# Strassen jobs in another product order over six PSUM banks, two gate/up tiles ahead instead of four, and a new table of kept-back halves

## The chip, the cores and the metric

One Trainium2 chip, one core of it. The metric is device time in microseconds (us) of one execution of the kernel; a median of several runs is compared. TensorE multiplies, VectorE (DVE in the profile) and GpSimd (POOL) work element by element, ScalarE (ACT) evaluates functions and copies, SyncE (SP) issues most of the transfers. "us" is microseconds throughout.

## The reference, cut to what matters

```python
x = A_x                                   # (1, 2048, 512)
xn = layernorm(x)
# A: attention, 32 heads of 16
qkv = xn @ wqkv                           # 512 x 1536
p = softmax(q @ k.T * 16 ** -0.5)         # per head, 2048 x 2048
s = (p @ v).reshape(1, 2048, 512) @ wo
# B: SwiGLU
h = silu(xn @ w_gate) * (xn @ w_up)       # 512 x 1792
g = silu(h @ w_down)                      # 1792 x 512
return x + s * g
```

## The kernel before, in words

The 2048 tokens are four blocks `b` of 512 columns; the 1792 hidden features of B are 14 tiles `f` of 128 (`GROUPS`: tiles 0 to 6 and 7 to 13). A product in near-float32 precision is three matmuls in the type fp32r: high part by high part, low by high, high by low. So every operand is split: ScalarE casts the high part, VectorE subtracts it to get the low part (`whole_of`, `summed_of`, `split_turn`, `split_gu`).

The program has two halves.

**Prologue.** Tokens are normalised and turned, and the values of all blocks and the queries and keys of blocks 0 and 1 are made in plain products (`value_tile`, `feature_tile`). In `value_tile` the twelve matmuls of a tile run chunk by chunk `c`: high·high, low·high, high·low. The queries and keys of blocks 2 and 3, and the gate and up products of the tiles in `AHEAD` for blocks 2 and 3, come from `strassen(i)`, one call per job of the list `jobs`. A job is a 2 x 2 block product in seven products of six matmuls instead of eight products: a pair of query or key tiles (`("qk", pair)`) or one gate/up tile (`("f", f)`), for the two token blocks at once. `product(bank, left, right, start, stop)` issues six matmuls into a PSUM bank; four of the products open a bank, three are added to a bank that is already open. In between, ScalarE copies two of the partial sums to SBUF (`m1`, `m5`), VectorE and GpSimd make the sums `w`, `u3`, `c12`, `c21`, `c22`, and the operands of the next job are split (`sums`, `whole_of`, `summed_of`). In each job the four banks are four tiles of the pool `pps`, and the products run in the order bank 0, bank 1, bank 0 again, bank 2, bank 3, bank 2 again, bank 3 again. The second product into bank 0 has to follow ScalarE's copy `m1` of it, and so on.

A "qk" job ends in four calls of `feature_out`: ScalarE squares (L972) and casts (L973) a 128x512 result, VectorE or GpSimd subtracts (L974) into a tile `parts` (pool `p3`, four buffers), SP stores it (L976), and VectorE keeps a running maximum `top` (L977). Two of the four calls are put off into the next job (`behind`). An "f" job ends in ScalarE's Tanh and VectorE's products into `g1` and `g2` and two stores to `h_d` (L1039, L1044). `bound` multiplies the eight maxima `top` by a small matrix (L820, the "squares") and reduces the two banks; `spread_shift` turns the sum, makes a flag and a shift from it; `first_loads` issues twenty loads of the first keys, values and queries on SP's queue (L186, L203). They are hung into the middle of jobs through the argument `between`. `fill(n)` issues `n` steps of the feed-forward part: a step is a pair of 64-row matmuls side by side (L291). After the last job stands `fill(3 * DC)`, 24 steps, which is the whole first gate unit. Then every engine reads the flag and branches around a general path (`tc.If`, L1132).

**Attention.** `plan()` cuts the 32 units (a group of four heads and a token block, 16 key tiles each) into blocks of `k` key tiles (2 to 6), and gives each block a number `n` of feed-forward steps; it is a cheapest path over a cost per block, whose ends are the ends of the feed-forward units of `SEQUENCE`. In a block, TensorE makes the scores (L1224), ScalarE the exponentials (L1227 for both halves at once, L1234 for one half), the feed-forward steps lie in between, and `values` (L526) multiplies the block before by the values. `SHARED[(k, n)]` lists, for one kind of block, the pairs of which one half is kept back: VectorE copies that half out of PSUM (L1231), and ScalarE exponentiates it from SBUF at the block's end (L1244). The second entry of `SHARED` says after which pair how many steps are issued.

Feed-forward units are gates (24 steps, one tile `f` for one block) and downs (21 steps). For blocks 2 and 3 the tiles in `AHEAD` are left out of `SEQUENCE` and loaded from `h_d` by `load_hidden`. `split_gu` makes the operands of the next gate, `load_gu` loads the one after.

SP issues its transfers in the order of the program; each engine works through its own instructions in order too.

Of the kernel before, what the change touches and what calls it, by code (L numbers as in the profile page):

```python
# [19 lines left out]
P = 128  # L20
# [21 lines left out]
AHEAD = (0, 1, 7, 8)  # L42


def sequence():
# [87 lines left out]
def tile_block(ctx: ExitStack, tc: tile.TileContext, x, xcols, wqkv, wo, w_gate, w_up, w_down, out):  # L133
# [166 lines left out]
    def gate_unit(i, b, f, then):  # L300
        if i + 1 < len(gates):
            split_gu(i + 1)
        if i + 2 < len(gates):
            load_gu(i + 2)
        hi, lo = gu.pop(i)
        n = 0
        for c in range(DC):
            for wt, j in ((hi, 0), (hi, 1), (lo, 0)):
                both(wt[:, c], fx[:, j, c], n == 0, n == 3 * DC - 1)
                n += 1  # L310
                if n == 3 * DC:
                    th = one.tile([P, TB], F32, tag="th", name="th")
                    ga = two.tile([P, TB], F32, tag="ga", name="ga")
                    act(th, bankx, AF.Tanh, scale=0.5)
                    dve.scalar_tensor_tensor(ga, th, 1.0, bankx, op0=ALU.add, op1=ALU.mult)
                    dve.scalar_tensor_tensor(ga, ga, 0.5, banky, op0=ALU.mult, op1=ALU.mult)
                    kept.append((f, ga))
                    if now >= 0:
                        split_kept()
                    then()  # L320
                if n == DC:
                    split_wd()
                if n in (12, 20):
                    split_hidden()
                yield
# [273 lines left out]
    with ExitStack() as pro:  # L599
# [281 lines left out]
        def value_tile(b, t):  # L881
            xh, xl = xt[b % 2]
            order = None
            if b == 0:
                parts = [slice(i, i + 1) for i in range(3)] if t == 1 else [slice(0, 3, 2), slice(1, 2)]
                order = [(i, part) for part in parts for i in range(DT)]
                if t == 1:
                    order.insert(11, (partial(turn_x, 0, 2), None))
# [30 lines left out]
        for at, pair in zip((0, 1, 3, 5), (0, 2, 1, 3)):  # L919
            jobs.insert(at, ("qk", pair))  # L920
# [58 lines left out]
        behind = []  # L979

        def strassen(i, between=None):
# [4 lines left out]
            m1, w, m5, u3, c12, c21, c22, g1, g2 = spots  # L986
# [10 lines left out]
            bank = [pps.tile([P, 512], F32, tag="ps", name="ps") for _ in range(4)]  # L997
            more = i + 1 < len(jobs)
# [3 lines left out]
            nc.scalar.copy(m1, bank[0])  # L1002
            while behind:
                behind.pop(0)()
            product(bank[1], summed[1], t2, True, True)
# [3 lines left out]
            product(bank[0], whole[2], b21, False, True)  # L1009
            if kind == "f":  # L1010
                act(g1, bank[0], AF.Tanh, scale=0.5)
                dve.scalar_tensor_tensor(g1, g1, 1.0, bank[0], op0=ALU.add, op1=ALU.mult)
            else:
                feature_out(2 * f, 2, bank[0], False)
# [9 lines left out]
            else:  # L1024
                split_gu(0)
# [4 lines left out]
            product(bank[2], summed[3], b22, False, True)  # L1030
            dve.tensor_add(c12, bank[2], w)
            if kind == "f":
                act(g2, c12, AF.Tanh, scale=0.5)
            else:
                feature_out(2 * f, 3, c12, False)
            if kind == "f":
                dve.scalar_tensor_tensor(g2, g2, 1.0, c12, op0=ALU.add, op1=ALU.mult)
                dve.scalar_tensor_tensor(g2, g2, 0.5, c22, op0=ALU.mult, op1=ALU.mult)
                sp.dma_start(h_d[1, f], g2)  # L1039
            product(bank[3], whole[0], t4, False, True)  # L1040
            dve.tensor_add(c21, bank[3], w)
            if kind == "f":
                dve.scalar_tensor_tensor(g1, g1, 0.5, c21, op0=ALU.mult, op1=ALU.mult)
                sp.dma_start(h_d[0, f], g1)  # L1044
            else:
                behind.append(partial(feature_out, 2 * f + 1, 3, c22, True))
                behind.append(partial(feature_out, 2 * f + 1, 2, c21, False))
# [6 lines left out]
        step(28, 0, dve.tensor_sub, upper_x, upper_x, lower_x)  # L1054
        step(28, 1, split_turn, 0, upper_x)
        step(29, 0, split_turn, 1, lower_x)
        step(29, 0, whole_of, 0)
# [8 lines left out]
        for b in range(NB):  # L1066
# [4 lines left out]
            for n, (make, i) in enumerate(slots):  # L1071
# [10 lines left out]
                if at == 26:  # L1082
                    dve.memset(acc, 0.0)
# [18 lines left out]
        spots = [spots[:, i] for i in range(4)] + [xin[:, i] for i in range(4)] + [wide_mr[:, 0]]  # L1102
        def spread_shift():
            nc.tensor.transpose(extra[0:1, :P], sm, ident)
            dve.reduce_max(s4, extra[0:1, :P], axis=AX.X)
# [59 lines left out]


# [176 lines left out]
```

## Time and profile before

| | |
|---|---|
| median of 3 runs | 1408.86 us (1408.38 to 1410.98) |
| the profiled execution | 1408.27 us, of it 1406.5 us span |
| TensorE | busy 98% of the span, mean granted clock 0.992 |
| ScalarE, VectorE, GpSimd | busy 84%, 58%, 11% |
| first Strassen product | at 102.86 us |
| first score | at 209.08 us |

Two times lie around a span: the span counts from the first to the last instruction of the program, the run's time some 1.8 us more. In the views a row reads: start, duration, engine, line, operation, out<-in, count, and in brackets how long the engine had stood idle and what ended that. "PEclk" is the granted share of TensorE's clock. A busy TensorE in the table of engines is not one at its peak, since the matmuls overlap; distances between starts say more.

### The profile page before, as it was taken

How to read it: one execution, taken by the hardware profiler on the slowest of the kernel's cores; microseconds unless marked ns; L12 is line 12 of the kernel's file. 1: busy time of each engine (PE TensorE's matmuls, PEld its weight loads, DVE VectorE, ACT ScalarE, POOL GpSimd, SP SyncE). 2: the span in 40 equal slices, each digit the busy share in tenths (PEclk: the TensorE clock that was granted, in tenths of full speed). 3: DMA queues.
4: the chain of work that ended last, by engine and by line, in shares of the span. 5: the costliest groups of instructions: out<-in, count | busy, mean ns of one | idle time of the engine just before them, and what ended most of it. 6: DMA issues, size and time to landing. Idle time of an engine off the chain costs nothing.

```text
span 1406.5 us, 27374 instructions
## 1 busy us (share of the span) xinstructions
PE 1383.1 (98%) x10912; PEld 845.4 (60%) x10912; DVE 820.4 (58%) x1296; ACT 1181.3 (84%) x1971; POOL 157.4 (11%) x192
## 2 busy tenths in 40 slices
PE   9998979999999999999999999999999999999998
PEld 7876756565655556555656565555555565565655
DVE  7697855653644655455646554555556445556656
ACT  6746618889988998999899999999998989989885
POOL 4235620000000000000010100000100000000142
PEclk9999989999999999999999999999999999999999
DMA  9888657254324443434543446246433113225652
GB/s 305 271 273 247 179 146 176 66 110 104 88 64 111 117 103 78 105 83 106 114 109 97 99 104 140 57 90 144 93 67 87 35 38 77 58 74 148 212 179 86
DMA packets 141908, 170.18 MB, mean 121 GB/s; under 512 B 13913, under 2 KB 85617, under 8 KB 141006
## 3 DMA queue, kind: packets, MB, share of 16 engines
q1 hardware_dynamic: 134238, 143.04, 40.6%
q0 software_dynamic: 7056, 24.78, 5.4%
q8 instruction: 88, 1.44, 0.4%
q10 hardware_dynamic: 480, 0.54, 0.1%
q14 instruction: 46, 0.38, 0.1%
HBM read 119.78 MB, written 46.41 MB: 118 GB/s over the span
## 4 chain that ended last, share of the span: by engine, by line
PE 81%; ACT 3%; DVE 1%; issue 0%; DVEq 0%
PE acc L526 30%; PE bankx L291 24%; PE score L1224 9%; PE single L1224 8%; PE banky L291 7%; ACT pr L1234 1%; ACT pr L1244 1%; PE spare L1224 1%; ACT pr L1227 1%; DVE pr L1231 0%; DVE y L296 0%; PE spare L1279 0%; ACT th L295 0%; PE banky L1279 0%; DVE gul L221 0%
## 5 line engine op out<-in xcount | busy, mean ns | idle before, releaser
L526 PE MATMUL acc<-pr,vst 128*17 128x512 f32 x4096 | 460.2, 593 | 0.0
L1234 ACT ACTIVATE pr<-single 128x512 f32<-128x512 f32 x675 | 388.2, 607 | 17.2 <-PE single L1224 10.5
L1227 ACT ACTIVATE pr<-score 128x1024 f32<-128x1024 f32 x335 | 345.9, 1033 | 31.6 <-PE score L1224 19.9
L526 PEld LDWEIGHTS acc<-pr,vst 128*17 128x17 f32 x4096 | 109.7, 97 | 282.5 <-issue 280.1
L291 PE MATMUL bankx<-fx,guh 64*128 64x512 f32 x768 | 254.9, 394 | 3.7 <-PEq L1132 3.7
L291 PE MATMUL banky<-fx,guh 64*128 64x512 f32 x768 | 254.6, 393 | 0.0
L1231 DVE COPY pr<-spare 128x512 f32<-128x512 f32 x177 | 122.3, 691 | 221.4 <-PE spare L1224 203.2
L1244 ACT ACTIVATE pr<-pr 128x512 f32<-128x512 f32 x419 | 230.2, 641 | 0.0
L1224 PE MATMUL score<-qst,kst 50*128 50x512 f32 x847 | 228.8, 418 | 1.4 <-SPq L1132 1.4
L1231 DVE COPY pr<-single 128x512 f32<-128x512 f32 x242 | 166.5, 688 | 97.6 <-PE single L1224 96.4
L1224 PE MATMUL single<-qst,kst 50*128 50x512 f32 x917 | 218.9, 398 | 0.7 <-DVE pr L1231 0.6
L291 PE MATMUL bankx<-wd,hh 64*128 64x512 f32 x672 | 200.1, 392 | 0.0
L291 PE MATMUL banky<-wd,hh 64*128 64x512 f32 x672 | 199.7, 392 | 0.0
L1224 PEld LDWEIGHTS score<-qst,kst 50*128 50x128 f32 x847 | 103.0, 184 | 130.2 <-ACT pr L1234 94.6
L1234 ACT ACTIVATE pr<-score 128x512 f32<-128x512 f32 x177 | 106.1, 599 | 71.9 <-PE spare L1224 58.2
L291 PEld LDWEIGHTS bankx<-fx,guh 64*128 64x128 f32 x768 | 143.7, 187 | 21.8 <-issue 4.7
L291 PE MATMUL bankx<-fx,gul 64*128 64x512 f32 x384 | 151.3, 394 | 0.0
L291 PE MATMUL banky<-fx,gul 64*128 64x512 f32 x384 | 151.3, 394 | 0.0
L291 PEld LDWEIGHTS banky<-fx,guh 64*128 64x128 f32 x768 | 143.8, 187 | 2.8
L1224 PEld LDWEIGHTS single<-qst,kst 50*128 50x128 f32 x917 | 115.6, 185 | 29.1 <-ACT pr L1234 12.3
L291 PEld LDWEIGHTS bankx<-wd,hh 64*128 64x128 f32 x672 | 124.4, 186 | 13.0
L291 PEld LDWEIGHTS banky<-wd,hh 64*128 64x128 f32 x672 | 125.2, 186 | 3.4
(262 smaller groups left out, 1838.8 us busy)
## 6 DMA issues: line engine op xcount, KB each, us to landing
fx<-xt_d SPq DMA_DIRECT2D x48, 512.0 KB
kst<-k_d SPq DMA_DIRECT2D x192, 64.0 KB
qst<-q_d SPq DMA_DIRECT2D x192, 64.0 KB
gur<-in_B_w_gate_dram SPq DMA_DIRECT2D x48, 256.0 KB
gur<-in_B_w_up_dram SPq DMA_DIRECT2D x48, 256.0 KB
q_d<-parts SPq DMA_DIRECT2D x16, 512.0 KB
k_d<-parts SPq DMA_DIRECT2D x16, 512.0 KB
xt_d<-xt POOLq DMA_DIRECT2D x6, 1024.0 KB, 6.5
```

The lines of the kernel that those rows point to most:

```text
L291: mm(bank, lhs[h], rhs[h], start=start, stop=stop)
L526: mm(acc[h * 32:h * 32 + DH + 1], v[:, kt % CT, h * (DH + 1):(h + 1) * (DH + 1)], probs[2 * i + h // 2][:, h % 2], start=tiles[0] == at == ...
L1224: mm(banked[h], k[r, j, kc * P:(kc + 1) * P], q[r, j], start=True, stop=True)
L1227: exps.append(act(pr, both_banks, AF.Exp, scale=0.25))
L1231: dve.tensor_copy(pr[:, h], banked[h])
L1234: exps.append(act(pr[:, h], banked[h], AF.Exp, scale=0.25))
L1244: exps.append(act(part, part, AF.Exp, scale=0.25))
```

## The change

Two tiles, 0 and 7, are computed ahead instead of four, so the job list shrinks from eight jobs (qk, qk, f, qk, f, qk, f, f) to six (qk, qk, f, qk, qk, f), and `SEQUENCE` gains a gate unit each for tiles 1 and 8 of blocks 2 and 3. The seven products run as bank 0, 1, 2, 3, then 0, 2, 3 again, over a ring of six banks: four of `pps`, `extra` and `acc`. Three of the four `feature_out` calls of a "qk" job are put off. In the last job the gate unit 0 is issued in two halves of 12 steps between its fifth product and its last two, `bound` and `spread_shift` lie in this job, and what is left of its results (`first_half`, `second_half`) follows after the branch. `first_loads` moves from job 5, the last "qk" job, to job 3, the last but one, and in the new order it stands ahead of that job's own four results. `acc` is zeroed after the branch. `value_tile` takes high·high and high·low of all chunks first in the first tile of blocks 2 and 3. The table `SHARED` is new.

```diff
-AHEAD = (0, 1, 7, 8)
+AHEAD = (0, 7)
 SHARED = {
-    (2, 6): ((), (0, 0, 1, 5)),
     (3, 9): ((2, 3), (0, 0, 0, 3, 2, 4)),
-    (4, 15): ((2, 5), (0, 0, 1, 3, 3, 2, 2, 4)),
-    (5, 18): ((2, 3, 5, 6, 7), (0, 0, 1, 2, 3, 2, 2, 2, 2, 4)),
-    (5, 21): ((3, 4, 5, 6, 7), (0, 0, 2, 3, 1, 3, 4, 0, 4, 4)),
-    (5, 24): ((2, 3, 7), (0, 0, 0, 4, 1, 5, 5, 2, 3, 4)),
-    (6, 21): ((2, 3, 4, 5, 7, 8, 9), (0, 0, 1, 2, 2, 1, 3, 2, 2, 1, 3, 4)),
+    (4, 15): ((2, 4, 5), (0, 0, 1, 3, 3, 1, 3, 4)),
+    (5, 18): ((2, 3, 5, 6, 7), (0, 0, 3, 1, 3, 2, 2, 1, 2, 4)),
+    (5, 21): ((2, 3, 7), (0, 0, 1, 2, 2, 5, 2, 3, 2, 4)),
+    (5, 24): ((2,), (0, 0, 1, 2, 4, 2, 5, 3, 2, 5)),
+    (6, 21): ((2, 4, 5, 7, 8, 9), (0, 0, 0, 3, 3, 1, 3, 2, 2, 1, 3, 3)),
     (6, 24): ((2, 5, 7, 8, 9), (0, 0, 0, 3, 3, 3, 2, 3, 2, 2, 2, 4)),
 }
 ...
     def gate_unit(i, b, f, then):
-        if i + 1 < len(gates):
+        if 0 < i < len(gates) - 1:
             split_gu(i + 1)
 ...
         def value_tile(b, t):
-            if b == 0:
-                parts = [slice(i, i + 1) for i in range(3)] if t == 1 else [slice(0, 3, 2), slice(1, 2)]
+            if b == 0 or b > 1 and t == 0:
+                parts = [slice(i, i + 1) for i in range(3)] if b == 0 and t == 1 else [slice(0, 3, 2), slice(1, 2)]
 ...
-        for at, pair in zip((0, 1, 3, 5), (0, 2, 1, 3)):
+        for at, pair in zip((0, 1, 3, 4), (0, 2, 1, 3)):
             jobs.insert(at, ("qk", pair))
 ...
         def strassen(i, between=None):
-            bank = [pps.tile([P, 512], F32, tag="ps", name="ps") for _ in range(4)]
+            if not ring_of:
+                free = [pps.tile([P, 512], F32, tag="ps", name="ps") for _ in range(4)]
+                homes_of = {(4 * len(jobs) - 4) % 6: extra, (4 * len(jobs) - 1) % 6: acc}
+                ring_of.extend(homes_of[n] if n in homes_of else free.pop(0) for n in range(6))
+            bank = [ring_of[(4 * i + n) % 6] for n in range(4)]
 ...
             if more:
                 sums(i + 1)
             product(bank[0], whole[1], b11, True, False)
-            nc.scalar.copy(m1, bank[0])
+            product(bank[1], summed[1], t2, True, True)
             while behind:
                 behind.pop(0)()
-            product(bank[1], summed[1], t2, True, True)
+            nc.scalar.copy(m1, bank[0])
             dve.tensor_add(w, bank[1], m1)
             if more:
                 whole_of(i + 1)
-            product(bank[0], whole[2], b21, False, True)
-            ... (the results of bank 0)
+            else:
+                split_gu(0)
             product(bank[2], summed[0], t1, True, False)
             nc.scalar.copy(m5, bank[2])
             if between:
                 between()
             product(bank[3], summed[2], t3, True, False)
             ... (u3, c22, summed_of(i + 1), load_raw or load_gu)
+            if more:
+                product(bank[0], whole[2], b21, False, True)
+                if kind == "f":
+                    first_half()
+                else:
+                    feature_out(2 * f, 2, bank[0], False)
+                product(bank[2], summed[3], b22, False, True)
+                other_half()
+                product(bank[3], whole[0], t4, False, True)
+                second_half()
+                if kind != "f":
+                    behind.append(partial(feature_out, 2 * f + 1, 3, c22, True))
+                    behind.append(partial(feature_out, 2 * f, 3, c12, False))
+                    behind.append(partial(feature_out, 2 * f + 1, 2, c21, False))
+            else:
+                product(bank[2], summed[3], b22, False, True)
+                other_half()
+                fill(3 * DC // 2)
+                spread_shift(ring_of[(4 * i + 4) % 6])
+                split_gu(1)
+                fill(3 * DC // 2)
+                product(bank[0], whole[2], b21, False, True)
+                product(bank[3], whole[0], t4, False, True)
+                behind.append(first_half)
+                behind.append(second_half)
 ...
-                if at == 26:
-                    dve.memset(acc, 0.0)
 ...
-            strassen(i, {0: partial(store_x, 2), 1: partial(store_x, 3), 5: first_loads, 6: bound, 7: spread_shift}.get(i))
-        fill(3 * DC)
+            strassen(i, {0: partial(store_x, 2), 1: partial(store_x, 3), 3: first_loads, len(jobs) - 1: bound}.get(i))
         fast = nc.values_load(flag, min_val=0, max_val=1)
 ...
+        while behind:
+            behind.pop(0)()
+        dve.memset(acc, 0.0)
```

`first_half` is Tanh and one VectorE operation on bank 0 into `g1`, `second_half` is the sum `c21` and for an "f" job one more product and the store of `g1`; `other_half` is the sum `c12`, and for an "f" job Tanh, two products and the store of `g2`.

More of the change, by code (lines that the diff above doesn't have):

```diff
@@ L995, in product, with first_half, second_half, other_half @@
                         n += 1
[L997 to L998 removed]
+            def first_half():
+                act(g1, bank[0], AF.Tanh, scale=0.5)
+                dve.scalar_tensor_tensor(g1, g1, 1.0, bank[0], op0=ALU.add, op1=ALU.mult)
+            def second_half():
+                dve.tensor_add(c21, bank[3], w)
+                if kind == "f":
+                    dve.scalar_tensor_tensor(g1, g1, 0.5, c21, op0=ALU.mult, op1=ALU.mult)
+                    sp.dma_start(h_d[0, f], g1)
+            def other_half():
+                dve.tensor_add(c12, bank[2], w)
+                if kind == "f":
+                    act(g2, c12, AF.Tanh, scale=0.5)
+                    dve.scalar_tensor_tensor(g2, g2, 1.0, c12, op0=ALU.add, op1=ALU.mult)
+                    dve.scalar_tensor_tensor(g2, g2, 0.5, c22, op0=ALU.mult, op1=ALU.mult)
+                    sp.dma_start(h_d[1, f], g2)
             if more:
@@ L1029, in strassen @@
                 load_gu(i + 3 - len(jobs))
[L1030 to L1033, printed above, removed]
-            else:
[L1035 to L1047, printed above, removed]
+            if more:
+                product(bank[0], whole[2], b21, False, True)
+                if kind == "f":
+                    first_half()
[9 more added lines that the diff above has]
+                    behind.append(partial(feature_out, 2 * f + 1, 2, c21, False))
+            else:
+                product(bank[2], summed[3], b22, False, True)
[8 more added lines that the diff above has]
+                behind.append(second_half)
         lower_x, upper_x = xin[:, :2], xin[:, 2:]
@@ L1101, in tile_block, with spread_shift @@
         spots = pc.tile([P, 4, TB], F32, tag="vl", name="spots")
[L1102 to L1105, printed above, removed]
+        spots = [spots[:, i] for i in range(4)] + [xin[:, i] for i in range(4)]
+        def spread_shift(to):
+            nc.tensor.transpose(to[0:1, :P], sm, ident)
+            dve.reduce_max(s4, to[0:1, :P], axis=AX.X)
             dve.tensor_scalar(s4, s4, 0.51, None, op0=ALU.mult)
```

17 lines of the change are left out of this document (8 added, 9 removed).

## The prediction

> **What bounds the kernel now.** I read the page first, then busy time by stretch, then TensorE's waits in the prologue, last the timeline around them. Attention, by stretch (columns: length; busy time of TensorE, its weight loads, VectorE, ScalarE, GpSimd; granted clock, DMA share, GB/s):
>
> ```profile
> 300.00:500.00 200.00, 200.00 (x1708) 116.00 (x1705) 102.43 (x157) 181.75 (x304) 7.20 (x12) 1.00 0.43 99
> ```
>
> TensorE has no hole there, at full clock; ScalarE stands at 91%. Two pieces of the chain that ended last:
>
> ```profile
> 341.55 5.28 PE acc L526 x48
> 355.54 5.28 PE acc L526 x48
> ```
>
> Blocks of six key tiles with 24 steps (the planner's kind (6, 24)) repeat every 13.99 us, 5.28 of it `values`. The prologue is different; a row is one job, the last one is gate unit 0 and the branch:
>
> ```profile
> 102.86:116.64 13.78, 11.54 (x44) 8.96 (x43) 9.13 (x11) 5.49 (x9) 1.75 (x1) 0.88 0.73 200
> ...
> 138.54:148.28 9.74, 9.74 (x44) 7.87 (x42) 8.90 (x14) 4.75 (x9) 5.83 (x6) 1.00 0.69 217
> 148.28:159.06 10.78, 9.94 (x43) 7.81 (x42) 8.64 (x13) 6.56 (x11) 6.98 (x7) 1.00 0.78 204
> ...
> 180.99:197.40 16.41, 12.63 (x46) 9.26 (x44) 8.53 (x16) 2.92 (x5) 2.61 (x3) 0.79 0.60 172
> 197.40:209.08 11.68, 6.60 (x54) 4.89 (x53) 6.03 (x9) 0.60 (x1) 3.78 (x4) 0.93 0.38 105
> ```
>
> ```profile
> PE ps L993 <- ACT spots L1016: 4.8, 2, 3.8
> PE bankx L291 <- PEq L1132: 3.7, 1, 3.7
> PE ps L993 <- DVE spots L1020: 2.5, 3, 0.9
> PE ps L993 <- ACT spots L1002: 2.2, 1, 2.2
> ```
>
> The undisturbed fourth job takes 9.74 us for 42 matmuls, 0.232 each. The eight take 94.5 us (102.86 to 197.40) where 77.9 would do. The waits (total, times, longest) say why: a second product into a bank waits for the copy or sum of the first (L1002, L1016, L1020), and after a long wait the clock is down (0.88, 0.79). So a matmul or step costs 0.232 us everywhere, and the prologue's waits are the stock from which something can be gained.
>
> **The change part by part.** *Two jobs out, four gate units in.* Out: 2 x 9.74 = 19.5 us. In: 4 x 24 = 96 steps. In the block above 13.99 - 5.28 - 12 score slots x 0.232 leaves 5.93 for 24 steps; 5.57 are the steps, 0.36 the block's own overhead. So +22.3 us, and nothing covers it, since TensorE is the engine without holes.
>
> *The planner.* Worked through with the new list, `plan()` gives 103 blocks instead of 107, and 357 kept-back halves instead of 419. Four overheads less: -1.4. Kind (6, 21) falls from 15 blocks to 5, (5, 21) rises from 14 to 27, (5, 24) from 3 to 9. In a (6, 21) block the chain runs from ScalarE's and VectorE's work into a score:
>
> ```profile
> 702.48 0.92 ACT pr L1227
> ...
> 710.09 0.61 DVE pr L1231
> 710.74 0.50 PE spare L1224
> ```
>
> The score at 710.74 waits for the copy; I put such a wait at 0.3 us (half the copy), an estimate, and ten blocks fewer at -3. Bounds: -6 (the whole copy each) and +22 (the second rival). The new gates' splits and Tanh lie under TensorE (VectorE is busy 102 of 200 us). Attention: +22.3 - 1.4 - 3 = +17.9.
>
> *First tile of block 2.* Its low parts are now needed after eight matmuls.
>
> ```profile
> 80.00 0.50 PE L815 MATMUL ps<-vh,xt 128*128 128x512 f32 x1 [1.61 <-DVE xt L743]
> ...
> 81.14 0.73 PE L815 MATMUL ps<-vh,xt 128*128 128x512 f32 x1 [0.17 <-DVE xt L743]
> 81.66 0.63 PE L815 MATMUL ps<-vl,xt 128*128 128x512 f32 x1
> ```
>
> The last low part still comes at 81.1, so the last matmul starts there and not at 81.7: the first job starts 0.6 us earlier, at 102.3. Bounds: 0 and 1.8, the two waits together.
>
> *Six banks, new order.* A second product into a bank now comes four products (5.6 us) after the first. The waits on `spots` were for one copy or sum; the longest that no late transfer made was 2.2, so 5.6 covers them. What is late next: VectorE, filled to 8.6 to 8.9 of 9.74 us a job, which makes the next operands. I leave 0.3 for it (bounds 0 and 1.1 a job, the excess of the fifth job, as the third rival).
>
> *`first_loads` in job 3.* This step speaks against the change. In program order SP now has job 2's stores, the twenty loads, the load of gate 0, and only then the four stores of job 3's `parts`. Before:
>
> ```profile
> 164.07 0.34 SPq L1044 DMA_DIRECT2D h_d<-facc x1
> 166.27 0.37 SPq L976 DMA_DIRECT2D k_d<-parts x1
> 166.69 3.20 SPq L186 DMA_DIRECT2D kst<-k_d x6
> ...
> 177.00 0.73 SPq L213 DMA_DIRECT2D gur<-in_B_w_gate_dram x1
> 177.78 0.62 SPq L213 DMA_DIRECT2D gur<-in_B_w_up_dram x1
> ```
>
> An "f" job's last store is issued 5.0 us into the next job (164.07 against 159.06); 0.4 later the loads start and take 10.3 (166.69 to 177.00), the gate's 1.4. So the first `parts` store goes out 17.1 us into job 3, 7.4 into job 4. How long a store holds its buffer in so full a queue:
>
> ```profile
> 184.71 0.34 SPq L1044 DMA_DIRECT2D h_d<-facc x1
> ...
> 190.89 0.60 ACT L1011 ACTIVATE facc<-ps 128x512 f32<-128x512 f32 x1 [7.66 <-DMA h_d<-facc]
> ```
>
> 6.2 us. `parts` has four buffers; the fifth cast, job 4's first result, is wanted at about 7.7 (six products after five are 7.0, then a square) and waits until 13.6, which is 3.9 into the last job. Behind it on ScalarE stand that job's three put-off results, and after their last maximum come the squares of `bound`:
>
> ```profile
> 172.39 0.63 ACT L972 ACTIVATE sq<-facc 128x512 bf16<-128x512 f32 x1 [0.39 <-DVE facc L1041]
> 172.93 0.60 ACT L973 CAST parts<-facc 128x512 fp32r<-128x512 f32 x1
> ...
> 175.41 0.38 PE L820 MATMUL banky<-top,ind 128*32 128x512 bf16 x1 [0.45 <-DVE top L977]
> ```
>
> A square and a cast take 1.15 (172.39 to 173.53), so ScalarE's last cast starts 3.9 + 0.6 + 3 x 1.15 - 0.6 = 7.4 into the last job, and 2.5 later (172.93 to 175.41) the last square can go: 9.9. TensorE is there after three products, at 4.2. I take 5.6 us of waiting; bounds 0.4 (this wait before) and 7.7 (ScalarE's longest wait for a store).
>
> *The clock.* Before, the last long wait left the clock at 0.79 over 16.41 us, which is 3.4 lost. I take 2.5 for the new one, since part of it falls into idle time; bounds 0 and 3.4. The Trainium skill, "TensorE: Matmul & The Clock Gate", Part 1, says that the clock falls to half after an idle window of some 3.4 us, free-running. By that rule a wait broken into pieces under 3.4 us would cost nothing, and the sum would be 2.5 lower. The trace differs: the 2.2 us wait on L1002 was followed by a job at 0.88, and I go by the trace.
>
> *Gate 0 and the branch.*
>
> ```profile
> 202.85 0.39 PE L291 MATMUL bankx<-fx,gul 64*128 64x512 f32 x1
> ...
> 206.96 0.46 PE L291 MATMUL bankx<-fx,guh 64*128 64x512 f32 x1 [3.72 <-PEq L1132]
> ...
> 209.08 0.99 PE L1224 MATMUL score<-qst,kst 50*128 50x512 f32 x2 [1.36 <-SPq L1132]
> ```
>
> The steps stay 24 x 0.232 = 5.6. The branch holds TensorE 4.1 (202.85 to 206.96), then come two steps (0.5) and before, a wait of 1.4 for SP. Now the shift's transfers go out 24 matmuls before the branch, so SP is there first: 4.6, bounds 4.6 and 6.2. What is put off behind the branch (one Tanh, three VectorE operations and the zeroing) costs nothing: it is done while TensorE is in the branch and its first scores; without that cover it would be one Tanh of 0.6 and four VectorE operations of 0.6, 3.0.
>
> **The sum.** First job to first score, new: 6 x 9.74 = 58.4; steps 5.6; squares and the small transpose 0.7; branch 4.6; job 0 and operands 0.3; gate 0 waiting for the two reductions 0.4; squares 5.6; clock 2.5. Together 78.1, before 106.2: -28.1. With the earlier first job -28.7, with attention +17.9: -10.8. Against the profiled execution's 1408.27 that is 1397.5; the median of the runs, 1408.86, lies 0.6 above that execution, so the forecast is 1398.0.
>
> **The rivals.** *The stores land in time.* No TensorE or ScalarE row of the jobs before names a `parts` store, which speaks for it; that SP never had twenty loads ahead of them there speaks against it. Then the 5.6 and the 2.5 go: 1390.
>
> *The new table starves TensorE (the other side).* In the 27 (5, 21) and 9 (5, 24) blocks two halves fewer are kept back, 72 in all. Each holds its PSUM until ScalarE's 0.92 (L1227) is over and no longer VectorE's 0.61 (L1231). If TensorE waits for every such difference, 72 x 0.31 = +22, hence 1420, slower. It decides from 10.8/72 = 0.15 us a half on. For it: ScalarE is at 91%. Against: 96 more steps in the same exponentials lower that share, and the fourth to eighth pairs get more steps. A third of it, +7, gives 1405.
>
> *VectorE bounds the jobs.* If banks only move the wait, each of the first five jobs costs 10.78 as the fifth did: +5.2, less the 0.3: 1403. Against: the fourth job was VectorE's fullest here (8.90) and had no wait.
>
> **How the numbers follow.** The SP queue as summed: 0.50 (alone 1394 to 1402, from the ends of squares and clock). Stores in time: 0.22. VectorE: 0.10. The table by a third: 0.10, by more: 0.08. The range 1387 to 1405 leaves out the last, part of the third of the table, and a corner below. A change of 0.2% is 2.8 us, about what a measurement tells from nothing: faster (under 1406) 0.87, within it 0.06, slower 0.07.
>
> **What would show it.** Right: first score near 180; jobs 0 to 4 near 9.8 each without waits on `spots`; ScalarE waiting some 5 us for `q_d<-parts` around the last job's start, squares waiting for `top`; attention from first score on 18 longer. Wrong: no such wait (1390), a job row with VectorE at its length, or waits of scores on L1227 throughout attention.

## The result, and the profile after

| | before | after |
|---|---|---|
| median | 1409.26 us (1408.38 to 1410.98) | 1397.37 us (1396.31 to 1398.84) |
| profiled execution, its span | 1408.27, 1406.5 | 1397.1, 1395.3 |
| first Strassen product | 102.86 | 101.58 |
| first score | 209.08 | 183.10 |
| first score to the end of the span | 1197.4 | 1212.2 |

The ratio is 0.9915 (95% interval 0.9898 to 0.9932): faster by 0.85%. The forecast was 1398.0 (1387 to 1405). In the profiles the prologue became 26.0 us shorter and attention 14.8 longer, together -11.2.

The busy time by stretch after, columns as in the prediction. Six rows are the six jobs (the last with gate 0 and the squares), the seventh is the branch up to the first score:

```profile
101.58:113.43 11.85, 9.97 (x44) 7.81 (x42) 9.13 (x11) 6.32 (x10) 3.05 (x3) 1.00 0.81 232
113.43:123.09 9.66, 9.66 (x43) 7.89 (x42) 9.37 (x16) 6.42 (x14) 7.10 (x8) 1.00 0.66 254
123.09:135.31 12.22, 9.94 (x43) 7.80 (x42) 7.39 (x13) 7.95 (x12) 5.91 (x6) 1.00 1.05 317
135.31:145.03 9.72, 9.72 (x44) 7.89 (x42) 8.88 (x14) 4.70 (x10) 6.56 (x7) 1.00 0.68 206
145.03:154.71 9.68, 9.68 (x43) 7.89 (x42) 8.91 (x12) 6.48 (x11) 6.47 (x6) 1.00 0.60 158
154.71:180.03 25.32, 20.64 (x100) 13.79 (x98) 15.24 (x27) 6.83 (x12) 3.41 (x4) 0.87 0.73 220
180.03:183.10 3.07, 0.72 (x5) 0.35 (x5) 0.89 (x2) 0.00 (x0) 0.38 (x1) 1.00 0.36 95
```

Three of the first five jobs run at the undisturbed 9.7. The other two carry one wait each, and the last job three and a stretch at half clock. TensorE's rows that waited, from its timeline:

```profile
106.41 0.50 PE L1002 MATMUL extra<-twh,part 128*128 128x512 f32 x1 [1.88 <-ACT vt L895]
131.05 1.65 PE L1002 MATMUL extra<-xt,whole 128*128 128x512 f32 x6 [2.28 <-ACT spots L1030]
159.19 0.50 PE L1002 MATMUL ps<-twh,part 128*128 128x512 f32 x1 [1.56 <-DVE parts L973]
163.74 0.58 PE L819 MATMUL banky<-top,ind 128*32 128x512 bf16 x1 [2.36 <-DVE top L976]
165.08 0.58 PE L819 MATMUL banky<-top,ind 128*32 128x512 bf16 x1 [0.76 <-DVE top L976]
181.38 0.46 PE L290 MATMUL bankx<-fx,guh 64*128 64x512 f32 x1 [1.35 <-PEq L1155]
183.10 0.77 PE L1250 MATMUL score<-qst,kst 50*128 50x512 f32 x2 [1.00 <-DVE facc L1008]
```

What stands behind the second to fifth is on SP's queue and on ScalarE (two views; L975 and L972 are a `parts` tile's store and cast, L971 its square, L1030 the copy `m1`):

```profile
148.11 2.76 SPq L185 DMA_DIRECT2D qst<-q_d x6
150.98 0.73 SPq L212 DMA_DIRECT2D gur<-in_B_w_gate_dram x1
151.76 0.61 SPq L212 DMA_DIRECT2D gur<-in_B_w_up_dram x1
152.48 3.23 SPq L975 DMA_DIRECT2D q_d<-parts x4
```

```profile
127.05 0.62 ACT L972 CAST parts<-facc 128x512 fp32r<-128x512 f32 x1 [2.32 <-DMA q_d<-parts]
129.89 0.62 ACT L972 CAST parts<-facc 128x512 fp32r<-128x512 f32 x1 [1.69 <-DMA q_d<-parts]
130.41 0.58 ACT L1030 COPY spots<-extra 128x512 f32<-128x512 f32 x1
...
157.83 0.58 ACT L972 CAST parts<-ps 128x512 fp32r<-128x512 f32 x1 [5.04 <-DMA q_d<-parts]
```

Job 3's first store goes out at 152.48, behind the loads and the gate's two transfers, and at 157.83 the cast that needs its buffer has stood 5.04 us. The same kind of wait, not foreseen, stands in job 2: two casts wait 2.32 and 1.69 for the stores of job 0, and the copy `m1` stands behind them. By the landings in the trace these stores, issued at 117.81 and 118.32, landed at 127.03 and 129.87: 9.2 and 11.6 us, beside the two 1 MB stores of the second `store_x` (issued 117.26 and 117.83, landed 123.21 and 126.83). The DMA share of that job is 1.05.

The last job around its half clock, cut into stretches of 3.41 us, half the length of the half clock itself (163.63 to 170.45):

```profile
156.80:160.21 3.41, 1.85 (x8) 1.22 (x7) 1.77 (x4) 1.11 (x2) 0.00 (x0) 1.00 1.06 300
160.21:163.63 3.42, 1.17 (x9) 0.31 (x8) 1.76 (x4) 2.58 (x5) 1.26 (x1) 1.00 1.09 320
163.63:167.04 3.41, 2.54 (x5) 1.26 (x5) 3.06 (x6) 1.31 (x3) 0.00 (x0) 0.50 1.06 386
167.04:170.45 3.41, 3.41 (x9) 2.64 (x8) 2.42 (x5) 0.00 (x0) 0.79 (x1) 0.50 0.52 202
```

A second stretch at half clock follows the branch in both kernels. Behind the first score it is 5.3 us long before and 3.4 after (one row of each):

```profile
209.08:214.35 5.27, 5.27 (x25) 5.27 (x27) 3.43 (x6) 2.84 (x4) 0.00 (x0) 0.50 0.79 192
```

```profile
184.11:187.52 3.41, 3.41 (x19) 3.14 (x18) 3.20 (x4) 2.42 (x4) 3.25 (x4) 0.50 0.61 191
```

Attention after, the same 200 us as before, and the group of ScalarE's late exponentials of kept-back halves (x is their number):

```profile
300.00:500.00 200.00, 200.00 (x1708) 119.50 (x1702) 104.18 (x158) 178.65 (x300) 9.85 (x17) 1.00 0.42 97
```

```profile
L1270 ACT ACTIVATE pr<-pr 128x512 f32<-128x512 f32 x357 | 198.2, 644 | 0.0
```

TensorE still has no hole; ScalarE fell from 91% to 89%. 357 halves are kept back, as worked out; before there were 419.

### The profile page after: what moved, and what is told of

It reads as the page before. It is cut to its first block, busy times and chain, and to the rows that moved or that the text cites. A ratio compares the mean times of both kernels' runs of the same rounds, so it can differ in the third digit from the quotient of the medians.

```text
span 1395.3 us, 27442 instructions
## 1 busy us (share of the span) xinstructions
PE 1376.7 (99%) x11020; PEld 854.3 (61%) x11020; DVE 777.1 (56%) x1228; ACT 1169.9 (84%) x1942; POOL 146.1 (10%) x182
## 4 chain that ended last, share of the span: by engine, by line
PE 87%; DVE 0%; DVEq 0%; issue 0%
PE acc L525 32%; PE bankx L290 29%; PE score L1250 10%; PE single L1250 9%; PE banky L290 6%; PE spare L1250 0%; PE spare L1305 0%; PE banky L1305 0%; PE score L1305 0%; DVE y L1312 0%; PE single L1305 0%; DVE facc L1008 0%; DVE y L1318 0%; DVEq L1365 0%
## 5 line engine op out<-in xcount | busy, mean ns | idle before, releaser
L1260 ACT ACTIVATE pr<-single 128x512 f32<-128x512 f32 x722 | 411.0, 607 | 9.4 <-PE single L1250 3.8
L1253 ACT ACTIVATE pr<-score 128x1024 f32<-128x1024 f32 x354 | 365.8, 1033 | 27.5 <-PE score L1250 11.0
L290 PE MATMUL bankx<-fx,guh 64*128 64x512 f32 x832 | 275.4, 393 | 1.4 <-PEq L1155 1.4
L290 PE MATMUL banky<-fx,guh 64*128 64x512 f32 x832 | 275.6, 393 | 0.0
L1257 DVE COPY pr<-spare 128x512 f32<-128x512 f32 x158 | 109.2, 691 | 227.7 <-PE spare L1250 211.8
L1270 ACT ACTIVATE pr<-pr 128x512 f32<-128x512 f32 x357 | 198.2, 644 | 0.0
L1257 DVE COPY pr<-single 128x512 f32<-128x512 f32 x199 | 136.9, 688 | 100.3 <-PE single L1250 98.5
L290 PEld LDWEIGHTS bankx<-fx,guh 64*128 64x128 f32 x832 | 155.3, 187 | 20.2 <-issue 2.2
L290 PE MATMUL bankx<-fx,gul 64*128 64x512 f32 x416 | 163.7, 394 | 0.0
L290 PE MATMUL banky<-fx,gul 64*128 64x512 f32 x416 | 163.6, 393 | 0.0
```

Source lines behind the costliest of these rows:

```text
L290: mm(bank, lhs[h], rhs[h], start=start, stop=stop)
L1253: exps.append(act(pr, both_banks, AF.Exp, scale=0.25))
L1257: dve.tensor_copy(pr[:, h], banked[h])
L1260: exps.append(act(pr[:, h], banked[h], AF.Exp, scale=0.25))
L1270: exps.append(act(part, part, AF.Exp, scale=0.25))
```

## The experiments

Twelve kernels. Each ratio is to runs of the kernel before on the same chip; "rest" is the span from the first score on. The intervals are some 0.17% to either side, 2.4 us, so a single edit of 1 to 2 us is read from its place in the trace and not from the ratio. "First score" and "rest" are of the one profiled execution of each kernel, which can lie apart from the median: in e9 it was the fastest of four (1392.54, the others 1395.65 to 1397.08), in e7 the slowest of ten (1408.38, the lowest 1405.39). Every rest holds the half clock behind the branch, between 3.4 us (the change) and 6.2 us (e5); with half of that length taken off, the ten kernels that have two tiles ahead and the new table lie between 1210.2 and 1210.8.

| kernel | median us | ratio, 95% interval | first score | rest |
|---|---|---|---|---|
| the change | 1397.37 | 0.9915, 0.9898 to 0.9932 | 183.10 | 1212.2 |
| e4 four tiles ahead | 1396.20 | 0.9919, 0.9903 to 0.9936 | 196.04 | 1197.4 |
| e6 four banks | 1396.20 | 0.9912, 0.9895 to 0.9928 | 181.43 | 1213.3 |
| e3 old table | 1398.92 | 0.9925, 0.9907 to 0.9944 | 182.43 | 1214.4 |
| e7 new table in the kernel before | 1406.36 | 0.9988, 0.9978 to 0.9997 | 211.25 | 1195.4 |
| e1 loads a job later | 1394.79 | 0.9907, 0.9891 to 0.9924 | 180.89 | 1212.9 |
| e9 loads a job earlier | 1395.87 | 0.9911, 0.9894 to 0.9927 | 178.74 | 1212.0 |
| e5 last value tile in `pps` | 1396.88 | 0.9915, 0.9899 to 0.9932 | 180.22 | 1213.3 |
| e2 five `parts` buffers | 1394.16 | 0.9903, 0.9886 to 0.9919 | 181.93 | 1212.6 |
| e10 three moves | 1395.43 | 0.9903, 0.9886 to 0.9919 | 180.53 | 1212.4 |
| e8 rest ahead of the branch | 1400.73 | 0.9947, 0.9930 to 0.9963 | 186.26 | 1212.8 |
| e11 three edits together | 1391.39 | 0.9877, 0.9860 to 0.9893 | 177.86 | 1212.4 |
| e12 fifth buffer in the jobs alone | 1389.38 | 0.9860, 0.9844 to 0.9877 | 175.35 | 1212.4 |

### Which part gave the gain: e4, e6, e3, e7

**e4** keeps order, banks, branch and first gate, but goes back to four tiles ahead and the old plan and table.

```diff
-AHEAD = (0, 7)
+AHEAD = (0, 1, 7, 8)
-        for at, pair in zip((0, 1, 3, 4), (0, 2, 1, 3)):
+        for at, pair in zip((0, 1, 3, 5), (0, 2, 1, 3)):
-            strassen(i, {..., 3: first_loads, len(jobs) - 1: bound}.get(i))
+            strassen(i, {..., 5: first_loads, len(jobs) - 1: bound}.get(i))
```

> The changed kernel with four tiles ahead again, the job order of before (qk, qk, f, qk, f, qk, f, f), first_loads in the last qk job, and the old table: the change without its fewer jobs. Two more jobs cost 19.4 us, attention is 14.8 shorter as it was before, and no cast of a later qk job follows the loads, so the last job's waits and slow clock (4.7 + 2.4) should be gone. Theory (order and banks took the waits, fewer jobs gave little): 1397.4 + 19.4 - 14.8 - 7.1 = about 1395. Rival (the fewer jobs are what made it faster): above 1402.

1396.2, the rest 1197.4 as before. Six of the eight jobs took 9.66 to 10.06; one wait of the kind of job 2 is left, and the first score waits for GpSimd, which fills two rows of `kst` with ones late (L177). From TensorE's timeline of e4:

```profile
130.29 1.66 PE L1003 MATMUL ps<-xt,whole 128*128 128x512 f32 x6 [3.32 <-ACT spots L1031]
...
196.04 0.99 PE L1251 MATMUL score<-qst,kst 50*128 50x512 f32 x2 [3.42 <-POOL kst L177]
```

So what e4 keeps brings the whole gain; two tiles fewer, with the plan and table that go with it, bring nothing that can be measured. They may even cost something: the wait of 3.42 is e4's own, where the change waits 1.00, so e4 without it would be up to 2.4 us faster, an estimate from these two rows. In e4's trace the first seven jobs take 71.7 us instead of 78.1, which is the order and the banks, and the last job with the gate and the branch takes 22.8 instead of 28.1.

**e6** takes the six banks away and keeps the order.

```diff
-                ring_of.extend(homes_of[n] if n in homes_of else free.pop(0) for n in range(6))
-            bank = [ring_of[(4 * i + n) % 6] for n in range(4)]
+                ring_of.extend(pps.tile([P, 512], F32, tag="ps", name="ps") for _ in range(4))
+            bank = list(ring_of) if more else [extra, *ring_of[1:3], acc]
```

> The changed kernel with the same four banks in every job, as before (the last job still uses the two others where results are read after the branch), but the new product order. Theory (the four products between the two uses of a bank are what takes the waits; a bank comes back a job later in time): within 2 us of 1397. Rival (the two additional banks are needed): the first product of each job waits for the results of the job before, about 1 us in each of five jobs and more where the clock falls, 1402 or above.

The jobs took 9.70, 10.25, 13.61, 9.81, 9.69, 22.87. TensorE waited 3.02 for the copy in job 2 (2.28 with six banks), and for VectorE's sums 0.36 once and 2.31 in the last job, where six banks wait 1.56 for VectorE's subtraction. Job 0 waits for nothing here, since its third bank is not `extra`: the 1.88 in the change comes from the ring itself. A second product four products after the first is enough; the ring bought no measurable time.

**e3** is the change with the old table, **e7** the kernel before with the new one.

```diff
 e3: SHARED as in the kernel before
 e7: SHARED as in the changed kernel, with (2, 6): ((), (0, 0, 1, 5)) kept
```

> The changed kernel with the old table of kept-back halves. From first score to end the change took 1212.2 us, 14.8 more than before, where the 96 steps alone are 22.3. Theory (the other mix of blocks gave the 7.5 back, not the table): priced by the mean excess of each kind of block before, the old table would cost 1 to 2 us more: attention 1213 to 1214, time 1 to 2 above the change. Rival (the table did it): attention up to 1219, time 6 above the change.

> The kernel before with the new table of kept-back halves (its own entry for the kind (2, 6) kept), nothing else. Theory (the table is a small gain and the smaller number of blocks and their mix gave the rest): attention 1 to 3 us shorter than the kernel before, the whole 1405 to 1407, the first score unchanged near 209. Rival A (the table is worth all of the 7.5 us that attention gained beside its added steps): 1401. Rival B (the table does nothing on the old plan): 1408 to 1409.

The rest went from 1212.2 to 1214.4 in e3, and from 1197.4 to 1195.4 in e7, whose whole is shorter by 0.12% (0.03 to 0.22). Twice 2 us: that is the table. (`plan()` does not read it, so the blocks are the same. The half clock behind the first score is 3.4 us in e3 as in the change, and in e7 4.5 where the kernel before has 5.3, which is 0.4 of e7's 2.0.) ScalarE's late exponentials in attention, before and in e7 (one row of each):

```profile
L1244 ACT ACTIVATE pr<-pr 128x512 f32<-128x512 f32 x419 | 230.2, 641 | 0.0
```

```profile
L1244 ACT ACTIVATE pr<-pr 128x512 f32<-128x512 f32 x391 | 215.7, 642 | 0.0
```

### The loads on SP's queue: e1, e9

```diff
-... 3: first_loads, len(jobs) - 1: bound}.get(i))
 e1: +... 4: first_loads, len(jobs) - 1: bound}.get(i))
 e9: +... 2: first_loads, len(jobs) - 1: bound}.get(i))
```

> The changed kernel with first_loads hung into job 4 instead of job 3, so that SP issues the four stores of job 3's parts ahead of the twenty loads. Theory (the stores stand behind the loads on SP, the fifth cast finds no free buffer): the waits of the last job (1.6 + 2.4 + 0.8 us) and its slow clock (about 2.4) go, the last job falls from 25.3 us to about 18, first score from 183.1 to about 176, the time from 1397.4 to about 1390. Rival (three put-off results a job are simply too much for ScalarE and VectorE): the squares still wait, the time stays within 1 us of 1397.

> The changed kernel with first_loads in job 2 instead of job 3: the four stores of job 3's parts are no longer behind them, and no transfers are pushed towards the branch, as they were with the loads in job 4 (DMA share 0.89 there instead of 0.35, and the branch held TensorE 3.4 us longer). Theory: the last job falls to about 18.5 us as it did with the loads in job 4, and the branch stays at about 3.5 us from the last matmul to the first score; first score about 176.5, 7 us less than the change: 1388 to 1390 beside a kernel before of 1407. Rival (what the last job loses less, the branch takes, wherever the transfers are, since the engines' code has to arrive): 1394 to 1396.

In both, job 3's stores no longer stand behind the loads, and the last job fell from 25.32 to 18.79 (e1) and 19.73 (e9), with one wait for the squares of 0.92 and 1.74 and no half clock. So the prediction's SP step holds, and its price roughly: 5.6 and 2.5 were summed, the last job lost 6.5 and 5.6. Both were expected to be 7 us faster than the change, and neither was. In e9's trace job 2 rose from 12.22 to 13.67, with 3.4 us of half clock behind its wait of 2.13, and the first score came 4.4 earlier; the median of its runs shows no gain. e1 lost the gain again at two places, seen in its stretches (job 0, last job, branch) and in TensorE's timeline:

```profile
101.38:114.83 13.45, 11.57 (x44) 8.97 (x43) 9.14 (x11) 6.50 (x10) 3.41 (x3) 0.87 0.71 203
...
155.64:174.43 18.79, 17.87 (x100) 12.36 (x98) 16.13 (x27) 6.13 (x11) 3.32 (x3) 1.00 0.82 231
174.43:180.89 6.46, 0.89 (x6) 0.36 (x5) 0.90 (x2) 0.00 (x0) 0.59 (x1) 0.88 0.68 202
```

```profile
178.91 0.47 PE L290 MATMUL bankx<-fx,guh 64*128 64x512 f32 x1 [4.48 <-PEq L1155]
```

The branch held TensorE 4.48 idle instead of 1.35, while DMA was busy 0.68 of the time instead of 0.36. And job 0, whose work is the same in both, fell to half clock behind the same wait of 1.88.

### The waits inside the jobs: e5, e2, e10

```diff
 e5: value_tile(..., extra if b == t == NB - 1 else None)  ->  value_tile(..., None)
 e2: p3 = ... bufs=4  ->  bufs=5   (row and shift moved into raw_x for the space)
 e10: e5, and {0: store_x(2), 1: store_x(3), 3: first_loads}  ->  {0: store_x(2), 2: first_loads, 3: store_x(3)}
```

> The changed kernel with only the last value tile moved from the bank extra into the pool. Theory: TensorE's wait of 1.9 us in job 0 goes, job 0 falls from 11.9 to about 10 us, the time by 1.9. Rival: ScalarE's copy of the first bank comes as late, the wait moves to the second product into it and job 0 stays above 11.5.

Job 0 fell to 9.69: its wait was for the last value tile's copy out of `extra`, the ring's third bank. But the store that job 2's copy stands behind lands when it lands: of the 2.2 us that job 0 gave, 1.1 came back in job 2, whose wait rose from 2.28 to 3.36. The first score came 2.9 earlier, and the median is the change's. e5, ScalarE and TensorE:

```profile
128.77 0.62 ACT L972 CAST parts<-facc 128x512 fp32r<-128x512 f32 x1 [1.55 <-DMA q_d<-parts]
```

```profile
129.93 1.66 PE L1002 MATMUL extra<-xt,whole 128*128 128x512 f32 x6 [3.36 <-ACT spots L1030]
```

> The changed kernel with five buffers for parts instead of four (the zero row and the shift move into dead rows of another tile to make the space). Theory: the fifth cast, job 4's first, waits no longer; the eighth waits for the landing of the third store instead of the fourth, so the squares go about 1.4 us earlier; in job 2 the last cast waits for a store that landed 2.8 us sooner, and its 2.3 us wait of TensorE goes. Together 3 to 4 us: about 1394. Rival (buffers are not what ScalarE waits for): 1397.

The wait in job 2 was gone (9.69), the last job 1.2 shorter; but the first job started at 106.31 instead of 101.58. VectorE and TensorE of e2:

```profile
82.14 0.69 DVE L764 TENSOR_TENSOR facc<-facc,spread 128x512 f32<-128x512 f32 x1 [2.56 <-DMA spread<-mr_d]
84.84 0.69 DVE L765 TENSOR_TENSOR facc<-facc,spread 128x512 f32<-128x512 f32 x1 [2.01 <-DMA spread<-mr_d]
```

```profile
95.30 1.65 PE L812 MATMUL ps<-vh,xt 128*128 128x512 f32 x3 [3.43 <-DVE xt L740]
```

> The same with two more moves: the last value tile goes into a bank of the pool instead of the bank extra, which is the third bank of job 0 (TensorE waited 1.9 us for its copy), and the two stores of 1 MB of block 3's columns are issued in job 3 instead of job 1, where parts stores took 9 to 12 us to land beside them (TensorE waited 2.3 us in job 2). Theory: 7 + 1.9 + 2.3 us less than the change, 1384 to 1386 here. Rival for the value tile: ScalarE copies late anyway and the second product of job 0 waits in its place (1.9 less of the gain). Rival for the stores: the twenty loads in job 2 take their place (2.3 less).

Jobs 0 to 2 took 9.70, 10.03 and 10.43, but job 4 12.64 (2.50 of waiting for the copy `m5`, L1037). On SP the last six of the twenty loads now took 5.49 to issue, beside the moved 1 MB stores, and the weights of the last job stood behind them: issued at 145.76 instead of 133.06. Two views, SP and ScalarE:

```profile
140.17 5.49 SPq L185 DMA_DIRECT2D qst<-q_d x6
145.76 0.40 SPq L929 DMA_DIRECT2D raw<-in_B_w_up_dram x1
```

```profile
149.51 0.83 ACT L950 CAST odd<-raw 128x768 fp32r<-128x768 f32 x1 [4.51 <-DMA raw<-in_B_w_gate_dram]
```

### What is put off behind the branch: e8

```diff
+        while behind:
+            behind.pop(0)()
+        dve.memset(acc, 0.0)
         fast = nc.values_load(flag, min_val=0, max_val=1)
         ...
-        while behind:
-            behind.pop(0)()
-        dve.memset(acc, 0.0)
```

> The changed kernel with what is put off behind the branch (the Tanh and the VectorE operations of gate unit 0, and the zeroing of facc's bank) put ahead of it again. Theory (the first score's 1.0 us wait for VectorE's read of the bank is the price of putting it off): that wait goes, last matmul to first score 2.5 to 3.0 instead of 3.5, the whole 0.5 to 1 us less. Rival (VectorE then reaches the branch later, by its three or four operations of about 0.6 us, and the score waits for that): last matmul to first score 4 to 6, the whole 1 to 2 us more.

Slower than the change by 3.4 us in the medians, with intervals that just overlap, and the first score comes 3.2 later; both theories missed the reason. The wait for VectorE went, but with the operations a store to `h_d` moved ahead of the branch, on SP (L1014), and SP came out of the branch last. e8, SP's and TensorE's timeline:

```profile
180.33 0.35 SPq L1014 DMA_DIRECT2D h_d<-facc x1
186.04 0.35 SPq L228 DMA_DIRECT2D wdr<-in_B_w_down_dram x1
```

```profile
186.26 0.99 PE L1250 MATMUL score<-qst,kst 50*128 50x512 f32 x2 [5.10 <-SPq L1158]
```

Between SP's two issues, from 180.68 to 186.04, lies its branch: 5.4 us, which could start only after the store. In the change SP's last issue before the branch ends at 177.5.

### Together: e11, e12

```diff
 e11: e5 and e2, and {0: both store_x, 2: first_loads, len(jobs) - 1: bound}
 e12: e11 with
-            parts = p3.tile(...)                                  # five buffers everywhere
+            parts = (p3 if used[0] % 5 else p6).tile(...)         # four, and a fifth in feature_out of the jobs
```

> The changed kernel with three of the edits tried singly put together: a fifth parts buffer, the last value tile in a bank of the four-buffer pool instead of extra, and the twenty loads hung into job 2; and both stores of the late xt blocks are hung into job 0, so that they are out of the queues before the parts stores of job 2. Theory (the waits are separate terms, each removed by its own edit): job 0 9.7 (was 11.8), job 2 9.7 to 10.5 (was 12.2), last job 19 to 20 with a squares wait below 2 and no half clock (was 25.3), branch 3.4; first score near 174 to 175 if the first job starts at 102, the whole 1389 to 1392. Rival (the transfers are a shared stock and a wait removed comes back at the next landing): some job among 1 to 5 shows a wait of 2 to 4 us on parts or on a copy behind it, or the branch takes 5 us or more; first score at 178 to 181, the whole 1394 to 1396.

> The kernel with the three edits together, but the fifth parts buffer is used in the jobs alone (each fifth product takes it), and the tiles of the blocks before turn over four buffers as in the changed kernel. Theory (with five buffers the blocks' stores went out earlier, stood ahead of the load of the spread mean and rate, and so the first job started at 105.5 to 106.3 instead of 101.6; it is that and not the fifth buffer in the jobs): VectorE does not wait for the spread, the wait for the last low parts of block 3 is 0.8 again instead of 3.4, the first job starts at 101.6 to 102.4, jobs 0 to 4 stay near 9.7 each, first score near 174, the whole 1387 to 1389. Rival (the late start has another cause, such as where the tiles lie, or the jobs' transfers, now earlier, meet another peak): the first job starts above 104, or a job or the branch is 2 to 4 us longer; the whole 1390 to 1393.

In e11 the first five jobs took 9.66 to 9.72 and the last 20.20, so these waits were separate terms. It started late, at 105.49, as e2 did, and the branch held TensorE 3.15. In e12 VectorE did not wait for the spread, and the first job started at 101.58: with five buffers in the blocks, two 512 KB stores of keys go out at 77.0 and 79.3 instead of 78.3 and 81.5, and the second load of the spread, issued at 75.9 (e2) or 75.3 (the change), lands after 8.8 us instead of 7.2. In e12 it took 6.7. e12 by stretch:

```profile
101.58:111.25 9.67, 9.67 (x44) 7.89 (x42) 8.49 (x10) 5.23 (x9) 2.20 (x2) 1.00 1.00 333
...
121.41:131.82 10.41, 9.96 (x43) 7.80 (x42) 10.09 (x14) 7.76 (x12) 7.21 (x7) 1.00 0.93 261
...
151.16:172.26 21.10, 19.20 (x100) 13.37 (x98) 17.51 (x29) 6.47 (x12) 4.46 (x4) 0.92 0.81 238
172.26:175.35 3.09, 0.75 (x6) 0.36 (x5) 0.90 (x2) 0.00 (x0) 0.39 (x1) 1.00 0.33 98
```

e12 beats both kernels: 1389.38, ratio 0.9860 with an interval wholly below the change's. It is a little above the expected 1387 to 1389. In its two dearer jobs (10.16 and 10.41) TensorE waits for VectorE's `u3`, 0.22 and 0.45 of the 0.5 and 0.7 that they take more; VectorE is fullest there.

## Why the prediction was right

The mechanism was right in its main parts, but that the whole came out 0.6 us from the forecast is luck, because its errors cancel: the prologue was taken 2.7 too short and attention 3.1 too long. Term by term:

| term | predicted | measured |
|---|---|---|
| start of the first job, earlier by | 0.6 | 1.3 |
| first job to first score | 78.1 | 81.5 |
| of it: jobs 0 to 4, above 9.74 each | 0.3 | 4.4 |
| waits in the last job before and at the squares | 5.6 | 4.7 |
| half clock | 2.5 | 2.8 |
| what else the last job takes beyond its matmuls | 0.4 | 1.8 |
| branch, start of the last matmul to first score | 4.6 | 3.5 |
| attention | +17.9 | +14.8 |

The half clock is the last job's 25.32 less the 18.79 that it takes in e1 (no half clock), less the difference of their waits (4.68 and 0.92). "What else" is e1's 18.79 less 9.74, 5.6, 0.7 and 0.92. Some 1.0 of it stands in e1's timeline where one kind of matmul follows another or its operand changes: ten starts there are 0.31 to 0.36 apart, not 0.23.

**The first job.** The last matmul of block 2's first tile started 1.0 earlier (80.65 instead of 81.66), where 0.6 was counted. Behind it the kernel before had a stretch of half clock, which the prediction did not see and the change lacks; at its end the change was 2.3 ahead (the 21st matmul from the tile's start began at 82.84 instead of 85.12). A new wait of 0.81 for the low parts of block 3 took most of the difference to 1.3 back. The half clock in the kernel before:

```profile
81.23:84.65 3.42, 3.42 (x9) 2.65 (x10) 3.35 (x7) 1.21 (x2) 0.44 (x1) 0.50 1.02 385
```

**Jobs 0 to 4: the step that failed.** The order did what was said of it: no job waited for a copy because of its distance. But "5.6 covers them" was said of the length of a copy, not of when it can start. Two copies started late: that of the value tile, which job 0's third bank waits for (1.88; e5 removes it), and `m1` in job 2, behind two put-off casts (2.28; e2 removes it). "Behind it on ScalarE stand that job's three put-off results" was worked out for job 4 and the last, and the same queue of three in jobs 1 and 2 was left out. The third rival, VectorE, gave 0.22 to 0.5 a job where it showed at all.

**SP's queue.** The first store 7.4 into job 4: it was 7.45 (152.48 less 145.03). It landed 5.3 later, for which 6.2 was taken. The rival that the stores land in time fell with the cast's 5.04. The three waits in the last job are 1.56, 2.36 and 0.76, together 4.7. e1 and e9 show that they come from `first_loads` in job 3.

**The clock.** In the prologue and behind the branch of every trace the half clock's stretches are 3.41 us or twice that, and in the change the next one begins 20.48 after the first (184.11 less 163.63), six times 3.41. The rows of the last job, cut in these windows, show when the clock falls: it fell behind the window in which TensorE was busy 1.17 of 3.42 us, and not behind the one before, which holds the wait of 1.56 and has TensorE busy 1.85. It came back behind a full window. Job 0's wait of 1.88 lies across two windows in the change and in one in e1, where the next is at half clock (two rows of the change, one of e1):

```profile
102.19:105.60 3.41, 2.34 (x11) 1.55 (x9) 2.53 (x3) 0.78 (x1) 0.00 (x0) 1.00 0.90 247
105.60:109.02 3.42, 2.61 (x11) 2.18 (x12) 2.69 (x3) 2.90 (x6) 0.00 (x0) 1.00 1.08 304
```

```profile
104.25:107.66 3.41, 1.53 (x7) 1.23 (x7) 2.30 (x4) 2.75 (x4) 0.00 (x0) 1.00 1.00 266
```

In the fourteen traces, from 60 to 225 us, every such window at full clock in which TensorE was busy for 0.45 of it or less was followed by half clock, and none with more than 0.58; between the two both happen. By the Trainium skill ("TensorE: Matmul & The Clock Gate", Part 1) the clock falls after an idle window of some 3.4 us, and the windows run freely. The traces agree with the length and with free running, but here a window that is about half idle is enough. So a wait in pieces is not free, as that rule had it in the prediction, and a wait of some 2 us costs nothing or some 2 us, by where it falls. The 2.5 holds for this run alone.

**The branch.** That TensorE would not wait for SP was right, and e8 shows what it hinges on: SP's last issue ahead of the branch. That the put-off work "costs nothing" was not: the first score waits 1.00 for VectorE's operation on the bank `extra` (L1008), which VectorE starts when it comes out of the branch itself. Ahead of the branch the score would come 3.2 later (e8).

**Attention.** The steps are 96 x 0.232 = 22.3 as before, so the rest gained 7.5 where 4.4 were summed. Of it 0.9 is no gain of the blocks: behind the first score the half clock is 5.3 us long before and 3.4 in the change, and costs half of that. The table is 2 (e3, e7). The other 4.6 come from four blocks fewer and another mix of kinds, which no experiment separated. The second rival had the sign wrong: TensorE shows no wait on a kept-back half in attention, and e7 gains.

**Fewer jobs.** That the sum's -19.5, +22.3 and the planner's share come out near zero was in the prediction only between the lines; e4 shows it, with its own wait on GpSimd. The gain was the prologue's waits, as the first part said.

## What to carry to other kernels

When an order removes waits for the length of a copy, ask next when each copy can start: what is put off ahead of it on its engine, and which transfer lets that go. Where transfers fill the queues, a wait taken away alone can come back in part at the next landing (e5, e10), or a store sent sooner can delay a load that matters more (e2). Taken singly, the edits that move a tile, a load or a buffer moved the ratio by 0.0012 at most, and moved together by 0.0055 (e12). Around a branch of all engines, look for the last instruction that each engine issues before it, SP too: in e8 the latest one set the start. And a wait of TensorE can cost a second time, at half clock, when it leaves a window of 3.4 us about half idle.

## What the runs showed of the hardware

- A branch around a large body has another price on each engine. TensorE's branch instruction took 4.6 to 5.4 us in twelve of the fourteen traces, 6.52 in e11 and 7.30 in e1. Matmuls that were still queued cover a part of it: TensorE was idle 1.35 in the change and in e12, 3.15 in e11, 4.48 in e1. From the branch to the next instruction VectorE took 2.8 to 3.1 us (5.8 in e1; in e8 its wait shows as 3.62 of idle time), SP 2.5 to 3.5, ScalarE and GpSimd 1.2 at most. The change's and e1's rows (the profile lists the instruction with TensorE's weight loads, as PEld):

```profile
L1155 PEldq COMPARE_BRANCH  x1: 4882/4882/4882, 176.3 to 176.3; - x1
```

```profile
L1155 PEldq COMPARE_BRANCH  x1: 7302/7302/7302, 171.4 to 171.4; - x1
```

  Over that instruction the DMA engines were busy 0.50 of the time in the change, 0.93 in e1 and 0.59 in e11, but 0.59 also in e7, where it took 4.74. That transfers slow it fits e1 and is not shown.
- The clock's half stretches are 3.4 us or a multiple, and follow a window of that length in which TensorE was idle for about half or more. One such stretch costs up to 1.7 us, and two in a row cost 2.8 in the change.
- A 512 KB store landed 3.4 us after its issue in job 0 (its first), with the DMA engines busy 0.41 of that time, and 11.6 us after it in job 2, with DMA at 1.05. How two queues share the engines there was not measured.
